# A Fourier mixing layer and its MLP on one core: the order of the one-channel loads, of the first sums and of the last results is changed

## The chip, the cores and the metric

One core of a Trainium2 chip runs the kernel. The metric is the time of one execution on the device in microseconds (us), as a median over runs. A core has four compute engines with an instruction queue each: TensorE (PE, matmul), VectorE (DVE), ScalarE (ACT) and GpSimd (POOL). SyncE (SP) only issues DMAs; ScalarE and POOL can issue DMAs too. Every queue is executed in order.

## The reference

```python
def reference(x, w_in, w_out):          # x: 8 x 3008 x 256, float32
    X = np.fft.fft(x, axis=1)           # along the sequence
    X = np.fft.fft(X, axis=2).real      # along the channels
    t = X.reshape(24064, 256)
    h = t @ w_in                        # 256 x 2048
    g = h * np.cos(h)
    return g @ w_out                    # 2048 x 256
```

## The kernel before, in words

*The channel DFT goes into the weights.* It is linear, so the kernel multiplies its matrices into `w_in` once: `fold_cos` and `fold_sin` (L293 to L306) make `Wc` and `Ws`, 128 x 2048 each, in four quarters of 512 columns. A quarter takes the two halves of `w_in` (`w1`, eight loads on SP's queue), two matmuls and one evacuation by ScalarE. Channel 128, the middle one, has a weight row of its own. It is row 127 of `Ws`. The step needs it as a column per 128 hidden units, so 16 DMAs of 128 elements turn it into `wex` (L299), four of them per quarter: those of quarters 0 to 2 on SP's queue, those of quarter 3 on ScalarE's.

*The sequence DFT is folded by symmetry.* For each batch, four tiles `xl0` to `xl3` (`load_x`, L169; `xl1` and `xl2` hold rows in reversed order and come by gathers on POOL's queue, `xl0` and `xl3` by three loads each on SP's) are added and subtracted into sums `e` and differences `o`, and these into `EO0` to `EO3` (`fold_x`, L325). VectorE does this for batch 0, POOL for the later batches, in small pieces (`FOLDS`) that stand between the steps below. A class `Dft` (L438) multiplies each `EO` by a constant matrix `MC`: `first` and `second` give two banks of PSUM, `side` copies half of one by ScalarE, `unfold` adds and subtracts on VectorE, and `plus` and `minus` (sums and differences) write the results for positions k and -k into rings of 8 tiles of 256 columns: `Rr` (real part), `Ir` (imaginary part). In each batch even and odd positions are separate DFTs (`R_even`, `I_even`, `R_odd`, `I_odd`).

*Channel 128 has its own ring `Rb`*, a single row spread over 128 partitions. For the even half of batch 0, `fold_first` (L380) spreads channel 128 of the loaded rows over 128 columns, and the DFT `x_even` gives `Rb` at once. For all the rest, `load_ext` (L540) reads channel 128 of all eight batches from DRAM, 4 bytes at a time, into `x1` (8 partitions x 768 elements, four times; five DMAs), writes it to DRAM as `xe_dr` and reads it back in tiles as `xs`. `fold_ext` (POOL) folds it, `clear_ext` and `dft_ext` run a small DFT of 28 matmuls between the steps, `ext_side` (ScalarE) copies the four groups out of PSUM, `ext_rows` makes one row per batch (VectorE the even half, POOL the odd half) and stores it to DRAM, and `spread_ext` loads a row into `Rb` with a broadcast DMA. `x1` and the row buffer share one tile (`rx`).

*The main work is 47 tiles of 256 positions (512 output rows), with 8 steps of 256 hidden units each: 376 steps.* The parts of step i are:
- `ext`: ScalarE writes `Rb` x `wex` into a PSUM bank `H`, two instructions (L661).
- `mm_P`, then `mm_Q`: four matmuls add `Wc` x `Rr` to it, four add `Ws` x `Ir`. `dbl` and `h_minus` give h for -k.
- `k_plus`, `k_minus`, `r_plus`, `r_minus`, two sines, `g_plus`, `g_minus`: h cos(h) in turns, on ScalarE and VectorE, into the tile `G`.
- `sum_1`, `sum_3`, `sum_2`, `sum_4`: four additions of 128 x 256 on POOL (`gtt`, L273).
- `mm_X1`, `mm_X2`: products with `w_out` or sums of its blocks (`WT`) into the banks `pA` to `pD`, which stand for a whole tile. Seven products serve for eight. The third product is the first that needs a POOL sum.

At the end of a tile `comb_copy`, `comb_1`, `comb_2`, `comb_22` and `comb_3` add the banks into `u` and `v`. `turn_u` and `turn_v` transpose these on VectorE, and `store` issues the output in pieces. For the last tile the stores go to SP's and ScalarE's queues in turns.

*The order.* Up to step 0 the program is written out by hand (before.py L943 to L979). From there each part is an event `at(time, function)`. A step's events stand PERIOD = 4.8 us apart (`T`), all events are sorted by time, and the functions run in that order. `pin` keeps an instruction in that program order on its engine. The loads of `load_x` and `spread_ext` are not pinned: the scheduler places them on SP's queue. The times only make the order, and the engines wait for each other by semaphores. The batch's folds begin at step 7 for batch 1; `load_ext` stands at -T, batch 1's `load_x` at -1.5 T, and the small DFT's events count from `e0`, 11 T.

The four helpers `mm` (L264), `vtt` (VectorE, L270), `gtt` (POOL, L273) and `act` (ScalarE, L276) issue most instructions, so the profile shows their lines.

Of the kernel before, what the change touches and what calls it, by code (L numbers as in the profile page):

```python
# [10 lines left out]
FP = mybir.dt.float32  # L11
# [4 lines left out]
ALU = mybir.AluOpType  # L16
# [3 lines left out]
ND = 256  # L20
# [83 lines left out]
def kernel(  # L104
# [45 lines left out]
    def gather_x(b, L, j, short):  # L150
# [13 lines left out]
            )  # L164
        )

    GATHERS = [(2, 0), (2, 1), (1, 0), (1, 1)]

    def load_x(b, gather=True):  # L169
        L = [  # L170
            spool.tile([128, 6 * ND], FP, tag=f"xl{j}", bufs=1, name=f"xl{j}")
            for j in range(4)
        ]
        if gather:
            for j, short in GATHERS:
                gather_x(b, L, j, short)
        for j, row in ((0, 0), (3, HALF)):
            nc.sync.dma_start(
                out=L[j][:, 0 : 4 * ND], in_=xrows(b, row, 4, 128, 4)
            )  # L180
            for h in range(2):
                nc.sync.dma_start(
                    out=L[j][64 * h : 64 * h + 64, 4 * ND :],
                    in_=xrows(b, row + 512 + 2 * h, 4, 64, 2),
                )
        return L
# [47 lines left out]

    Wc = cpool.tile([128, NDFF], FP, tag="Wc")
    Ws = cpool.tile([128, NDFF], FP, tag="Ws")
    wex = cpool.tile([128, NF], FP, tag="wex")

    halfpi2 = cpool.tile([128, 1], FP, tag="halfpi2")
    nc.vector.memset(halfpi2, 0.0)  # L240
# [35 lines left out]
        pin(nc.scalar.activation(out=o, in_=i, func=func, **kw))  # L276


    def fold_part(q, part, dst, tag):

        cols = slice(q * 512, (q + 1) * 512)
        ps = bank(tag)
        for h in range(2):
            mm(
                ps,
                CC[:, h * 256 + part : h * 256 + part + 128],
                w1_cols(h, q * 512, (q + 1) * 512),
                h == 0,
                h == 1,
            )  # L290
        act(dst[:, cols], ps)

    def fold_sin(q, tag="H"):  # L293
        fold_part(q, 128, Ws, tag)
        with nc.allow_non_contiguous_dma(reason="one row to columns"):
            for f in range(4 * q, 4 * q + 4):
                eng = nc.scalar if q == 3 else nc.sync
                pin(
                    eng.dma_start(  # L299
                        out=wex[:, f : f + 1], in_=Ws[127:128, f * 128 : (f + 1) * 128]  # L300
                    )
                )

    def fold_cos(q, tag="H"):
        fold_part(q, 0, Wc, tag)


    w2v = w2.rearrange("p (q c) -> p q c", c=ND)
# [71 lines left out]
    def fold_first(L):  # L380

        c = [t.rearrange("p (m d) -> p m d", d=ND)[:, :, 128:129] for t in L]
        c[1], c[2] = c[1][:, ::-1], c[2][:, ::-1]
        a = spool.tile([128, 6], FP, tag="xa", bufs=1, name="xa")
        g = spool.tile([128, 6], FP, tag="xg", bufs=1, name="xg")
        vtt(a.unsqueeze(2), c[0], c[1], ALU.add)
        vtt(g.unsqueeze(2), c[2], c[3], ALU.add)
        e = spool.tile([128, GW], FP, tag="G", bufs=3, name="xb")
        vtt(
            e[:, 0:768].rearrange("p (m d) -> p m d", d=128),  # L390
            a.unsqueeze(2).to_broadcast([128, 6, 128]),
            g.unsqueeze(2).to_broadcast([128, 6, 128]),
            ALU.add,
        )
        return e

# [39 lines left out]
            i += m  # L436

    class Dft:  # L438
        def __init__(self, ri, b, kodd, stat, ring=None, first=False):
            self.ri, self.b, self.kodd, self.stat = ri, b, kodd, stat  # L440
            self.n = NO if kodd else NE
            self.M = 127 if ri else 128
            self.first_only = first
            self.ring = ring if ring is not None else (Ir if ri else Rr)

        def mms(self, par, ps, start=True):
# [22 lines left out]
        def unfold(self):  # L469

            n = self.n
            self.ab = spool.tile([128, NE], FP, tag="ab", bufs=2, name="ab")
            n1 = n - 188
            u, v = self.uv[:, 0:NH], self.vs
            vtt(self.ab[:, 0:n1], u[:, 0:n1], v[:, 0:n1], ALU.add)
            u, v = (u, v) if self.ri == 0 else (v, u)
            vtt(self.ab[:, n - 1 : n - 189 : -1], u[:, 0:188], v[:, 0:188], ALU.subtract)
# [55 lines left out]
                )  # L533


    def spin(**kw):
        pin(nc.sync.dma_start(**kw))

    def load_ext():
        x1 = spool.tile([128, HALF + 1], FP, tag="rx", bufs=1, name="x1")  # L540
        xs = state["xs"] = spool.tile([128, 4, NB, 6], FP, tag="xs", bufs=1, name="xs")
        rows = [x1[j * NB : (j + 1) * NB] for j in range(4)]

        def copy(j, s0, s1, row, step):
            spin(
                out=rows[j][:, s0:s1],
                in_=bass.AP(
                    tensor=xt,
                    offset=x.offset + row * ND + 128,
                    ap=[[SEQ * ND, NB], [step * ND, s1 - s0], [1, 1]],  # L550
                ),
            )

        with nc.allow_non_contiguous_dma(reason="one channel, then runs of rows"):
            copy(1, 0, 1, 0, 1)
            copy(0, 0, 768, 0, 1)
            copy(1, 1, 768, SEQ - 1, -1)
            copy(2, 0, 768, HALF, -1)
            copy(3, 0, 768, HALF, 1)
            for j in range(4):  # L560
                spin(out=xe_dr[j], in_=rows[j][:, 0:768])
            for j in range(4):
                spin(
                    out=xs[:, j, :, 0:4],
                    in_=xe_dr[j][:, 0:512].rearrange("b (p m) -> p b m", m=4),
                )
                pairs = xe_dr[j][:, 512:768].rearrange("b (q h m) -> h q b m", h=2, m=2)
                for h in range(2):
                    spin(out=xs[64 * h : 64 * h + 64, j, :, 4:6], in_=pairs[h])
# [38 lines left out]

    def ext_rows(kodd, tt):
        n = NO if kodd else NE  # L610
        if not kodd:
            rx = spool.tile([128, HALF + 1], FP, tag="rx", bufs=1, name="rx")
            state["rx"] = rx[0:NB]
        rx, uv, b = state["rx"], state["side", 2 * kodd], state["side", 2 * kodd + 1]
        a = spool.tile([128, NE], FP, tag="ab", bufs=2, name="ab")[0:NB]
        n1 = n - 188
        u, v = uv[:, 0:NH], uv[:, NH:]
        tt(a[:, 0:n1], u[:, 0:n1], v[:, 0:n1], ALU.add)
# [37 lines left out]
    def ext(i):  # L656
        S = steps[i] = Step()
        S.H = bank("H")
        for j in range(2):
            f = 2 * (i % 8) + j  # L660
            act(S.H[:, j * TW : (j + 1) * TW], Rb[:, cols(i)], scale=wex[:, f : f + 1])  # L661

    def first_mm(i, W, ring, M):
        S = steps[i]
# [168 lines left out]
    def turn_v(q):  # L833
        turn(q, 2, tiles[q].v, 512, ((0, 0), (1, 1)))
        del tiles[q]

    def turn_u1(q):
        turn(q, 0, tiles[q].u[:, 0:TW], TW, ((1, 0),))

# [103 lines left out]
    for _ in range(8):  # L943
        mm(bank("M"), zero[:, 0:128], zero[:, 0:1].to_broadcast([1, 512]), True)
    sin(halfpi2)
    for q in range(2):
        fold_sin(q)
        fold_cos(q)
    EO, ops = fold_x(L_first, nc.vector, 1)

    def fold_now(keys):
        for key in keys.split():
            ops[key, 0]()

    R_even, I_even = Dft(0, 0, 0, EO[0]), Dft(1, 0, 0, EO[2])
    R_odd, I_odd = Dft(0, 0, 1, EO[1]), Dft(1, 0, 1, EO[3])

    fold_now("z1 z3 c0 e0 c3 e3 c2 e2 E2 x1 c1 e1 E0 EO0")
    fold_sin(2)
    fold_cos(2)  # L960
    R_even.first("pA")
    R_even.second("pB")
    xb = fold_first(L_first)
    fold_now("o0 o1 O0 o3 o2")
    R_even.side()
    x_even = Dft(0, 0, 0, xb, ring=Rb, first=True)
    x_even.first("pC")
    x_even.second("pD")
    R_even.unfold()
    R_even.plus()  # L970
    R_even.minus()
    fold_now("O2 EO2")
    I_even.first("pA")
    I_even.second("M")
    x_even.side()
    x_even.unfold()
    x_even.plus()
    x_even.minus()


    events = []
# [31 lines left out]
    for q in range(n_tiles):  # L1013
        t = (8 * q + 9) * T
        if q < n_tiles - 1:
            turns = ((2 * T + 1.0, turn_u), (3 * T + 1.0, turn_v))
        else:
            turns = ((4.3, turn_u1), (T + 1.15, turn_u2), (3 * T, turn_v))
        for dt, fn in (
            (1.45, comb_copy),  # L1020
            (4.2, comb_1),
            (T + 1.0, comb_2),
            (T + 1.1, comb_22),
            (T + 1.2, comb_3),
        ) + turns:
            at(t + dt, lambda fn=fn, q=q: fn(q))

# [27 lines left out]
    for t, fn in (  # L1055
        (-1.8, I_even.side),
        (-0.1, I_even.unfold),
        (0.0, I_even.plus),
        (0.1, I_even.minus),
        (0.95, lambda: fold_sin(3, "pD")),  # L1060
        (1.0, lambda: fold_now("EO1 EO3")),
        (3.0, lambda: fold_cos(3, "pA")),
        (3.1, lambda: R_odd.first("pB")),
        (3.2, lambda: R_odd.second("pC")),
        (T + 0.95, R_odd.side),
# [8 lines left out]
        (2 * T + 0.3, I_odd.minus),  # L1074
    ):
        at(t, fn)
    at(-T, load_ext)
    e0 = 11 * T
    at(e0 + 1.35, fold_ext)
    at(e0 + 2.905, clear_ext)  # L1080
    at(e0 + 4.75, dft_ext)
    for g in range(4):
        at(e0 + T * (1 + g // 2) + 1.46, lambda g=g: ext_side(g))
    at(e0 + 2 * T + 1.0, lambda: ext_rows(0, vtt))
    at(e0 + 3 * T + 1.35, lambda: ext_rows(1, gtt))
    at(e0 + 3 * T + 2.0, lambda: spread_ext(0, 1))
    fold_keys = [(k, p) for k in FOLDS for p in range(2 if k[0] not in "czx" else 1)]
    n_big = sum(k[0] not in "czx" for k, _ in fold_keys)
    for b in range(1, NB):
# [93 lines left out]
```

## Time and profile before

| | us |
|---|---|
| median of 5 runs | 1967.85 (1966.43 to 1976.26) |
| profiled execution | 1976.55 |
| its span | 1974.8 |
| TensorE busy | 1941.7 (98%) |
| first matmul of step 0 (`H<-Rr,Wc`) | 39.35 |
| small DFT of channel 128 (`H<-MC,xe`) | 113.11 |
| first `ext` from spread rows (`H<-Rb,wex` of step 16) | 140.59 |
| last `comb_3` | 1968.79 |

A line of the profile's timeline gives the start of a group of like instructions, its busy time, the engine, the line of the kernel, the operation, and `out<-in` by the names of the tiles with partitions x elements. The `x` at its end is the count. A bracket at the end, as in `[2.53 <-ACT H L276]`, is the time that the engine was idle just before the group, and what ended it. In a table by windows the columns after the window are its length, then busy time with the number of instructions of PE, DVE, ACT, POOL and weight loads, then the granted clock of TensorE (1 is full speed), the mean busy share of the core's 16 DMA engines, and GB/s. SPq is SP's DMA queue. A wait is put down to the releaser by semaphores, and a tile's name there can be that of another with the same semaphore.

### The profile page before, as it was taken

To read this page: it belongs to the slowest core of one execution; us is meant where nothing else is said; L and a number is where in the kernel's file an instruction comes from. 1 tells how busy PE (TensorE), PEld (TensorE's weight loads), DVE (VectorE), ACT (ScalarE), POOL (GpSimd) and SP (SyncE) were. 2 spreads that over 40 slices of the span, in tenths; PEclk is the share of its full clock that TensorE was granted. 3 is DMA by queue.
4 is the path that set the end of the run, shared out by engine and by line. 5 is a ranking of instruction groups with operands and counts; after the bars stand their busy time and mean duration, and the time that the engine had idled before them with its cause. 6 is when DMAs were issued, how large, how long until landed. Compare 5 with 4: busy or idle time off the path is not lost.

```text
span 1974.8 us, 28170 instructions
## 1 busy us (share of the span) xinstructions
PE 1941.7 (98%) x8855; PEld 1655.2 (84%) x8855; DVE 1417.4 (72%) x2348; ACT 1452.9 (74%) x2790; POOL 1349.8 (68%) x1853
## 2 busy tenths in 40 slices
PE   7989999999999999999999999999999999999998
PEld 4768888888888888888888888888888888887887
DVE  4657767777777767777677776777777776677777
ACT  1757767777777777777777776777777777777775
POOL 2767757776677766777677776677767776555654
PEclk9999999999999999999999999999999999999999
DMA  8821110111111011110210202002020110100101
GB/s 297 3 32 44 27 47 19 31 29 25 44 19 44 14 39 33 18 45 14 53 24 12 52 8 57 11 19 59 7 51 11 24 17 15 16 11 12 22 12 22
DMA packets 262401, 66.16 MB, mean 34 GB/s; under 512 B 249395, under 2 KB 252219, under 8 KB 262252
## 3 DMA queue, kind: packets, MB, share of 16 engines
q1 hardware_dynamic: 255916, 51.51, 14.9%
q0 software_dynamic: 3584, 12.58, 2.0%
q8 instruction: 70, 1.15, 0.3%
q14 instruction: 79, 0.65, 0.1%
q10 hardware_dynamic: 2752, 0.26, 0.1%
HBM read 39.48 MB, written 24.79 MB: 33 GB/s over the span
## 4 chain that ended last, share of the span: by engine, by line
PE 92%; DVE 3%; DMA 2%; ACT 2%; issue 1%; POOL 0%; SPq 0%; ACTq 0%; DVEq 0%; POOLq 0%
PE H L264 37%; PE pB L264 16%; PE pD L264 16%; PE pC L264 16%; PE pA L264 8%; DVE G L718 1%; ACT G L276 1%; DMA wex<-Ws 1%; DMA w<-in_moe_w_in_dram 1%; DVE v L270 0%; DVE G L270 0%; DVE M L270 0%; ACT E L276 0%; DVE ot L826 0%; DVE u L270 0%
## 5 line engine op out<-in xcount | busy, mean ns | idle before, releaser
L273 POOL TENSOR_TENSOR G<-G 128x256 f32<-128x256 f32 x1500 | 1079.2, 730 | 575.5 <-DVE G L718 473.0
L718 DVE SCALAR_TENSOR_TENSOR G<-H,G 128x512 f32<-128x512 f32 x376 | 257.0, 684 | 276.4 <-ACT G L276 276.4
L270 DVE TENSOR_TENSOR G<-H,G 128x512 f32<-128x512 f32 x376 | 260.0, 692 | 227.5 <-ACT G L276 224.4
L276 ACT ACTIVATE G<-H 128x512 int32<-128x512 f32 x376 | 224.6, 597 | 232.7 <-DVE G L270 231.3
L264 PE MATMUL H<-Rr,Wc 128*128 128x256 f32 x1504 | 388.5, 381 | 4.5 <-ACT H L276 4.4
L264 PE MATMUL pC<-G,WT 128*128 128x256 f32 x1504 | 387.9, 379 | 1.8 <-DVE u L270 1.6
L276 ACT ACTIVATE H<-Rb,wex 128x256 f32<-128x256 f32 x752 | 360.4, 479 | 39.0 <-DMA wex<-Ws 11.2
L264 PE MATMUL H<-Ir,Ws 127*128 127x256 f32 x1504 | 388.4, 380 | 0.7 <-ACT E L276 0.7
L276 ACT ACTIVATE E<-H 128x512 f32<-128x512 f32 x376 | 224.3, 596 | 207.4 <-PE H L264 204.7
L264 PEld LDWEIGHTS H<-Rr,Wc 128*128 128x128 f32 x1504 | 284.3, 190 | 53.7 <-ACT H L276 7.4
L264 PEld LDWEIGHTS pC<-G,WT 128*128 128x128 f32 x1504 | 284.5, 190 | 45.5 <-PE H L264 5.1
L264 PEld LDWEIGHTS H<-Ir,Ws 127*128 127x128 f32 x1504 | 283.0, 190 | 45.1 <-ACT E L276 6.1
L276 ACT ACTIVATE G<-G,halfpi 128x512 f32<-128x512 f32 x376 | 269.5, 717 | 1.5 <-DVE G L270 1.5
L270 DVE TENSOR_TENSOR G<-E,H 128x512 f32<-128x512 f32 x376 | 255.3, 679 | 5.3 <-PE H L264 3.4
L270 DVE TENSOR_TENSOR M<-G,M 128x512 f32<-128x512 f32 x376 | 257.7, 685 | 0.0
L718 DVE SCALAR_TENSOR_TENSOR G<-G,M 128x512 f32<-128x512 f32 x376 | 254.2, 676 | 0.4 <-ACT M L276 0.3
L276 ACT ACTIVATE M<-M,halfpi 128x512 f32<-128x512 f32 x376 | 246.4, 655 | 0.4 <-DVE M L270 0.3
L264 PE MATMUL pB<-G,WT 128*128 128x256 f32 x752 | 227.3, 384 | 2.4 <-POOL G L273 2.4
L264 PE MATMUL pA<-G,w 128*128 128x256 f32 x752 | 223.7, 379 | 2.4 <-issue 2.4
L276 ACT ACTIVATE M<-G 128x512 int32<-128x512 f32 x376 | 224.1, 596 | 0.0
L264 PE MATMUL pD<-G,WT 128*128 128x256 f32 x752 | 223.7, 379 | 0.0
L264 PE MATMUL pD<-G,w 128*128 128x256 f32 x752 | 223.7, 379 | 0.0
(129 smaller groups left out, 1788.3 us busy)
## 6 DMA issues: line engine op xcount, KB each, us to landing
out_dram<-ot SPq DMA_DIRECT2D x496, 32.0 KB
xl<-in_x_dram SPq DMA_DIRECT2D x16, 512.0 KB
xl<-in_x_dram SPq DMA_DIRECT2D x32, 128.0 KB
out_dram<-ot SPq DMA_DIRECT2D x256, 2.0 KB
MC<-dft_mats SPq DMA_DIRECT2D x4, 943.5 KB
Rb<-r SPq DMA_DIRECT2D x10, 376.0 KB
w<-in_moe_w_in_dram SPq DMA_DIRECT2D x4, 512.0 KB
w<-in_moe_w_out_dram SPq DMA_DIRECT2D x1, 2048.0 KB
```

The source lines that it names most:

```text
L264: nc.tensor.matmul(out_, lhsT=lhsT, rhs=rhs, start=start, stop=stop, skip_group_check=True)
L270: pin(nc.vector.tensor_tensor(out=o, in0=a, in1=b, op=op))
L273: pin(nc.gpsimd.tensor_tensor(out=o, in0=a, in1=b, op=op))
L276: pin(nc.scalar.activation(out=o, in_=i, func=func, **kw))
L718: nc.vector.scalar_tensor_tensor(out=o, in0=h, scalar=TWO_PI, in1=c, op0=ALU.mult, op1=ALU.mult)
```

## The change

It has seven parts.

1. *`wex`* becomes four tiles, one per quarter. Its copies come right behind each quarter of `Ws`: those of quarters 0 and 1 on ScalarE's queue, those of 2 and 3 on POOL's. The evacuation of `Wc`'s last quarter gets a time of its own (4.81).
2. *`fold_first`* adds channel 128 on VectorE in its small form and spreads it over 128 columns with ScalarE.
3. *Batch 0's DFTs*: `O2` and `EO2`, on which `I_even` waits, come ahead of `R_even`'s unfold; `o0` comes early; the sums (`plus`) of `R_even` and `x_even` stay ahead of step 0, while their differences, those of `I_even`, and `EO3` become events between 0.2 and 4.7. These two DFTs unfold into the buffers `xt0`, and the tile `ab` is a little wider.
4. *Eight warm matmuls* of zeros (`warm(8)`) stand behind the second quarter's fold.
5. *The one-channel loads*: `load_ext` stands at -1.5 T, ahead of batch 1's `load_x`, and its DRAM turn (`turn_ext`: `xe_dr`, then `xs`) at -T. `load_x`'s loads on SP are now pinned.
6. *The small DFT* begins a step later (`e0` = 12 T). The odd half goes first: VectorE makes its rows, its spread follows at once, and POOL makes the even half a step later.
7. *The last tile's* `v` is added, transposed and stored in two halves (`end_v`).

```diff
+    def spin(**kw):
+        pin(nc.sync.dma_start(**kw))
+
     def load_x(b, gather=True):
         for j, row in ((0, 0), (3, HALF)):
-            nc.sync.dma_start(
-                out=L[j][:, 0 : 4 * ND], in_=xrows(b, row, 4, 128, 4)
-            )
+            spin(out=L[j][:, 0 : 4 * ND], in_=xrows(b, row, 4, 128, 4))
             for h in range(2):
-                nc.sync.dma_start(
+                spin(
...
-    wex = cpool.tile([128, NF], FP, tag="wex")
+    wex = [cpool.tile([128, 4], FP, tag=f"wex{q}", name=f"wex{q}") for q in range(4)]
...
     def fold_sin(q, tag="H"):
-        fold_part(q, 128, Ws, tag)
-        with nc.allow_non_contiguous_dma(reason="one row to columns"):
-            for f in range(4 * q, 4 * q + 4):
-                eng = nc.scalar if q == 3 else nc.sync
-                pin(
-                    eng.dma_start(
-                        out=wex[:, f : f + 1], in_=Ws[127:128, f * 128 : (f + 1) * 128]
-                    )
-                )
+        ps = fold_mms(q, 128, tag)
+        act(Ws[:, q * 512 : (q + 1) * 512], ps)
+        eng = nc.gpsimd if q > 1 else nc.scalar
+        for f in range(4):
+            c = q * 512 + f * 128
+            pin(eng.dma_start(out=wex[q][:, f : f + 1], in_=Ws[127:128, c : c + 128]))
...
     def fold_first(L):
         vtt(a.unsqueeze(2), c[0], c[1], ALU.add)
         vtt(g.unsqueeze(2), c[2], c[3], ALU.add)
+        vtt(a, a, g, ALU.add)
         e = spool.tile([128, GW], FP, tag="G", bufs=3, name="xb")
-        vtt(
+        act(
             e[:, 0:768].rearrange("p (m d) -> p m d", d=128),
             a.unsqueeze(2).to_broadcast([128, 6, 128]),
-            g.unsqueeze(2).to_broadcast([128, 6, 128]),
-            ALU.add,
         )
...
+            tag = "xt0" if self.early else "ab"
+            self.ab = spool.tile([128, 2 * NH], FP, tag=tag, bufs=2, name=tag)
...
     def load_ext():
             copy(3, 0, 768, HALF, 1)
+            state["rows"] = rows
+
+    def turn_ext():
+        rows, xs = state["rows"], state["xs"]
             for j in range(4):
                 spin(out=xe_dr[j], in_=rows[j][:, 0:768])
...
     def ext_rows(kodd, tt):
-        if not kodd:
+        if kodd:
             rx = spool.tile([128, HALF + 1], FP, tag="rx", bufs=1, name="rx")
...
+    def end_v(q):
+        T = tiles[q]
+        for h in range(2):
+            c = slice(h * TW, (h + 1) * TW)
+            vtt(T.v[:, c], T.v[:, c], T.acc[3][:, c], ALU.add)
+            turn(q, 2 + h, T.v[:, c], TW, (((0, 0), (1, 1))[h],))
...
+    def warm(n):
+        w = bank("M")
+        for _ in range(n):
+            mm(w, zero[:, 0:128], zero[:, 0:1].to_broadcast([1, 512]), True)
+
     for q in range(2):
         fold_sin(q)
         fold_cos(q)
+    warm(8)
...
-    fold_now("z1 z3 c0 e0 c3 e3 c2 e2 E2 x1 c1 e1 E0 EO0")
+    fold_now("z1 z3 c0 e0 o0 c3 e3 c2 e2 E2 x1 c1 e1 E0 EO0")
...
-    fold_now("o0 o1 O0 o3 o2")
+    fold_now("o1 O0 o3 o2")
...
+    fold_now("O2 EO2")
     R_even.unfold()
     R_even.plus()
-    R_even.minus()
-    fold_now("O2 EO2")
...
     x_even.plus()
-    x_even.minus()
...
-            turns = ((2 * T + 1.0, turn_u), (3 * T + 1.0, turn_v))
+            turns = ((T + 1.2, comb_3), (2 * T + 1.0, turn_u), (3 * T + 1.0, turn_v))
         else:
-            turns = ((4.3, turn_u1), (T + 1.15, turn_u2), (3 * T, turn_v))
+            turns = ((4.3, turn_u1), (T + 1.15, turn_u2), (T + 1.2, end_v))
...
-        (0.1, I_even.minus),
-        (1.0, lambda: fold_now("EO1 EO3")),
-        (3.0, lambda: fold_cos(3, "pA")),
+        (1.0, lambda: fold_now("EO1")),
+        (1.1, I_even.minus),
+        (3.0, lambda: state.update(wc3=fold_mms(3, 0, "pA"))),
+        (4.81, lambda: act(Wc[:, 1536:2048], state.pop("wc3"))),
+        (0.2, R_even.minus),
+        (0.3, x_even.minus),
+        (4.7, lambda: fold_now("EO3")),
...
-    at(-T, load_ext)
-    e0 = 11 * T
+    at(-1.5 * T, load_ext)
+    at(-T, turn_ext)
+    e0 = 12 * T
...
-    for g in range(4):
-        at(e0 + T * (1 + g // 2) + 1.46, lambda g=g: ext_side(g))
-    at(e0 + 2 * T + 1.0, lambda: ext_rows(0, vtt))
-    at(e0 + 3 * T + 1.35, lambda: ext_rows(1, gtt))
-    at(e0 + 3 * T + 2.0, lambda: spread_ext(0, 1))
+    for n, g in enumerate((2, 3, 0, 1)):
+        at(e0 + T * (1 + n // 2) + 1.46, lambda g=g: ext_side(g))
+    at(e0 + 2 * T + 1.0, lambda: ext_rows(1, vtt))
+    at(e0 + 2 * T + 1.02, lambda: spread_ext(0, 1))
+    at(e0 + 3 * T + 1.35, lambda: ext_rows(0, gtt))
```

More of the change, by code (lines that the diff above doesn't have):

```diff
@@ L276, in act, with fold_mms @@
         pin(nc.scalar.activation(out=o, in_=i, func=func, **kw))
-    def fold_part(q, part, dst, tag):
-        cols = slice(q * 512, (q + 1) * 512)
+    def fold_mms(q, part, tag):
         ps = bank(tag)
@@ L290, in fold_part @@
             )
-        act(dst[:, cols], ps)
+        return ps
     def fold_sin(q, tag="H"):
-        fold_part(q, 128, Ws, tag)
-        with nc.allow_non_contiguous_dma(reason="one row to columns"):
-            for f in range(4 * q, 4 * q + 4):
-                eng = nc.scalar if q == 3 else nc.sync
-                pin(
-                    eng.dma_start(
-                        out=wex[:, f : f + 1], in_=Ws[127:128, f * 128 : (f + 1) * 128]
-                    )
-                )
+        ps = fold_mms(q, 128, tag)
[4 more added lines that the diff above has]
+            pin(eng.dma_start(out=wex[q][:, f : f + 1], in_=Ws[127:128, c : c + 128]))
     def fold_cos(q, tag="H"):
-        fold_part(q, 0, Wc, tag)
+        ps = fold_mms(q, 0, tag)
+        act(Wc[:, q * 512 : (q + 1) * 512], ps)
     w2v = w2.rearrange("p (q c) -> p q c", c=ND)
@@ L438, with __init__ @@
     class Dft:
-        def __init__(self, ri, b, kodd, stat, ring=None, first=False):
+        def __init__(self, ri, b, kodd, stat, ring=None, first=False, early=False):
             self.ri, self.b, self.kodd, self.stat = ri, b, kodd, stat
@@ L443, in __init__ @@
             self.first_only = first
+            self.early = early
             self.ring = ring if ring is not None else (Ir if ri else Rr)
@@ L471, in unfold @@
             n = self.n
-            self.ab = spool.tile([128, NE], FP, tag="ab", bufs=2, name="ab")
+            tag = "xt0" if self.early else "ab"
+            self.ab = spool.tile([128, 2 * NH], FP, tag=tag, bufs=2, name=tag)
             n1 = n - 188
@@ L533, in minus_sum @@
                 )
-    def spin(**kw):
-        pin(nc.sync.dma_start(**kw))
     def load_ext():
@@ L559, in load_ext @@
             copy(3, 0, 768, HALF, 1)
+            state["rows"] = rows
+    def turn_ext():
+        rows, xs = state["rows"], state["xs"]
+        with nc.allow_non_contiguous_dma(reason="runs of rows"):
             for j in range(4):
@@ L614, in ext_rows @@
         rx, uv, b = state["rx"], state["side", 2 * kodd], state["side", 2 * kodd + 1]
-        a = spool.tile([128, NE], FP, tag="ab", bufs=2, name="ab")[0:NB]
+        a = spool.tile([128, 2 * NH], FP, tag="ab", bufs=2, name="ab")[0:NB]
         n1 = n - 188
@@ L660, in ext @@
             f = 2 * (i % 8) + j
-            act(S.H[:, j * TW : (j + 1) * TW], Rb[:, cols(i)], scale=wex[:, f : f + 1])
+            act(S.H[:, j * TW : (j + 1) * TW], Rb[:, cols(i)], scale=wex[f // 4][:, f % 4 : f % 4 + 1])
     def first_mm(i, W, ring, M):
@@ L953, in fold_now @@
             ops[key, 0]()
-    R_even, I_even = Dft(0, 0, 0, EO[0]), Dft(1, 0, 0, EO[2])
+    R_even, I_even = Dft(0, 0, 0, EO[0], early=True), Dft(1, 0, 0, EO[2])
     R_odd, I_odd = Dft(0, 0, 1, EO[1]), Dft(1, 0, 1, EO[3])
-    fold_now("z1 z3 c0 e0 c3 e3 c2 e2 E2 x1 c1 e1 E0 EO0")
+    fold_now("z1 z3 c0 e0 o0 c3 e3 c2 e2 E2 x1 c1 e1 E0 EO0")
     fold_sin(2)
@@ L963 @@
     xb = fold_first(L_first)
-    fold_now("o0 o1 O0 o3 o2")
+    fold_now("o1 O0 o3 o2")
     R_even.side()
-    x_even = Dft(0, 0, 0, xb, ring=Rb, first=True)
+    x_even = Dft(0, 0, 0, xb, ring=Rb, first=True, early=True)
     x_even.first("pC")
     x_even.second("pD")
+    fold_now("O2 EO2")
     R_even.unfold()
     R_even.plus()
-    R_even.minus()
-    fold_now("O2 EO2")
     I_even.first("pA")
@@ L1023 @@
             (T + 1.1, comb_22),
-            (T + 1.2, comb_3),
         ) + turns:
```

## The prediction

> **What bounds the kernel now.** I read the page first, then who waited for whom on TensorE, then the timeline around each wait, the DMA share by window, and last the order of the built program on each queue.
>
> ```profile
> PE 1941.7 (98%) x8855; PEld 1655.2 (84%) x8855; DVE 1417.4 (72%) x2348; ACT 1452.9 (74%) x2790; POOL 1349.8 (68%) x1853
> ...
> PE H L264 <- POOL xe L273: 5.6, 1, 5.6
> PE H L264 <- ACT H L276: 4.4, 4, 2.5
> ```
>
> TensorE (PE) is busy 98% of the span; from 146 us to 1964 us a step without a DFT takes 4.75 us of matmuls, which this change does not touch. What it can win lies in the first 146 us and the last 7.
>
> ```profile
> 38.30 0.99 ACT L276 ACTIVATE H<-Rb,wex 128x256 f32<-128x256 f32 x2 [7.59 <-DMA wex<-Ws]
> 39.35 2.04 PE L264 MATMUL H<-Rr,Wc 128*128 128x256 f32 x4 [2.53 <-ACT H L276]
> ...
> 47.72 36.30 SPq L537 DMA_DIRECT2D x<-in_x_dram  x5
> ...
> 84.13 17.78 SPq L537 DMA_DIRECT2D xe_dr<-x  x4
> ...
> 84.81 0.19 POOL L351 COPY e<-xl 128x6 f32<-128x6 f32 x1
> 84.97 1.94 POOL L330 TENSOR_TENSOR e<-xl 128x381 f32<-128x381 f32 x2
> 86.87 3.02 POOL L273 TENSOR_TENSOR G<-G 128x256 f32<-128x256 f32 x4
> 89.87 0.59 PE L264 MATMUL pB<-G,WT 128*128 128x256 f32 x2
> ...
> 112.30 0.39 POOL L273 TENSOR_TENSOR xs<-xs 128x96 f32<-128x96 f32 x1 [6.42 <-DMA out_dram<-ot]
> 113.11 4.18 PE L264 MATMUL H<-MC,xe 128*8 128x189 f32 x28 [5.61 <-POOL xe L273]
> ...
> 140.59 0.99 ACT L276 ACTIVATE H<-Rb,wex 128x256 f32<-128x256 f32 x2 [4.39 <-DMA Rb<-r]
> ```
>
> Step 0 waits for the `wex` copies; step 12's small DFT waits for the one-channel data (the named `out_dram` shares a semaphore with `xs`); step 16 waits for the spread of `Rb`. The POOL rows at 84.81 fold batch 1's first tile, between the sums of steps 5 and 6.
>
> ```profile
> 38.00:40.00 2.00, 0.65 (x2) 0.57 (x3) 0.43 (x2) 1.20 (x3) 1.92 (x6) 0.85 0.82 230
> 50.00:52.00 2.00, 1.31 (x7) 0.83 (x6) 1.86 (x4) 2.00 (x6) 0.00 (x0) 1.00 0.19 1
> 52.00:62.00 10.00, 7.64 (x30) 5.85 (x29) 6.91 (x14) 5.59 (x11) 6.48 (x11) 0.89 0.91 3
> 84.00:98.00 14.00, 14.00 (x66) 12.29 (x66) 9.62 (x16) 10.96 (x22) 12.20 (x19) 1.00 0.96 2
> 100.00:102.00 2.00, 2.00 (x11) 1.73 (x11) 1.90 (x4) 1.35 (x3) 0.53 (x2) 1.00 0.02 6
> ```
>
> The last two columns are DMA share and GB/s: big loads fill the engines to about 40 us, then the one-channel stream holds them from 51 to 98.4, 47.4 us at 2 to 4 GB/s.
>
> **The change, part by part.** *The start.* Ahead of `EO2` VectorE loses `o0` (0.91, now in its idle time before 17.95), the spread (0.96, now ScalarE's: 0.6 for 512 columns in its rows, so 0.9 for 768, in a stretch where it idles 0.74 and the user at 27.18 is later) and `R_even`'s unfold, sums and differences (0.61 + 1.00 + 0.15, now behind). `EO2` moves from 33.3 to 29.8; `I_even`, free to start when `x_even`'s matmuls end at 30.84, gains 2.5; `Rb`'s sums are ready at 32.2, ScalarE's first step at 33.2, and step 0 follows `I_even` at 34.3 instead of 39.35. The differences (0.5 + 0.15 + 0.5), `EO3` (0.95) and `I_even`'s differences come later, in front of step 0's own VectorE work, where that engine idles 1.8 and 4.6 us. Step 3 is 4 to 6.5 us earlier; I take 5. The 8 warm matmuls cost 8 x 0.63 = 5.0 at half clock, 2.5 at full, in a 2.56 us gap; were they to overrun, `pA` still waits for VectorE until 24.2. The gap of 2.53 before 39.35 was followed by matmuls of 2.04 instead of 1.03, the one of 2.54 at 30.84 by no slow ones. The Trainium skill ("TensorE: Matmul & The Clock Gate", "Why this matters for your kernels") sees the clock drop after gaps of more than about 3 us; by that the warm matmuls would win nothing, and the sum would not move.
>
> *The copies of `wex`.* Twelve leave SP (26.03 to 40.9) for ScalarE (8) and POOL (4), and four go from ScalarE to POOL. ScalarE's eight take 0.74 each, 5.9 us, between 11.3 and 20, where it idles; its `Wc` evacuations queue behind them, which nothing needs before 19. POOL's take 0.95 each by its gather row (0.6 to 1.6): four inside its 22.5 us of idleness before 30, four more in its 13.0 us before 53.86. But each hardware DMA takes the next of eight completion semaphores and is not issued before that semaphore's last DMA has landed; two rows show it:
>
> ```profile
> SPq L225 <- DMA xl<-in_x_dram: 5.6, 3, 2.5
> SPq L299 <- DMA MC<-dft_mats: 4.3, 2, 2.5
> ```
>
> In the new order the fourth `w1` load on SP gets the semaphore of ScalarE's third copy, and the first `MC` load that of the fourth. So SP holds that load and all behind it until the copy, issued at 12.6, has landed; what is queued before keeps the engines busy to about 18.4, and data follow an issue by 1.9 (`xl`'s at 41.01 and 42.9). At the early end it lands as fast as the small `r` write at 134.90 (1.6 us), and nothing runs dry. At the late end the group, begun at 11.4, needs what SP's needed from 26.03 (12.2 us) and lands at 23.6: 23.6 + 1.9 - 18.4 = 7.1 us of hold. It has a queue of its own but saturated loads beside it (DMA share 1.0 to 34 us), so it lands when they thin out: I take 19.0, a hold of 2.5 us. The Trainium skill ("DMA: Bandwidth & Descriptors", "Issuing engines are not separate DMA queues") speaks against the move: another engine's queue saves issue time alone. By that the late end holds, and the sum below is 4.6 us worse. No row shows such a copy under this load.
>
> *Batch 1's rows behind the one-channel stream.* This is the part that decides. Both are on SP's queue, and the stream now comes first. Its start: big loads and gathers end at 40.1 today; minus 0.6 idle, plus 2.5 of hold, 42.0 (38 to 46.6). Its length: 47.4 (the four loads' issues were let through after 9.4, 11.1, 12.8 and 13.6 us; four at the first rate make 38, four at the last 55). It ends at 89.4. The first `xl` tile is three loads; SP issues them about 0.55 apart at the end, the last data come 1.9 after its issue: landed 2.9 later, 92.3. POOL wants it at 84.81 - 5 = 79.8. It is an in-order queue, so step 6's four sums stand behind that fold: copy and fold 2.1, three sums 2.2, and the third product of step 6, today at 89.87, runs at 96.7: +6.8. A gap of some 11 us then costs half clock for about 3.7 us after it, as after 113.11 and 39.35: +1.8. At that point the kernel is 8.6 us behind, whatever the start had gained.
>
> *The one-channel DFT.* The stream's data, today in `xs` 15 us after it ends, are there at 105, and the DFT, a step later, asks at 119: no wait. Step 11 starts at 102.40 and step 17 at 146.49, 44.1 us; six steps of 4.75 and the DFT at full clock (half of 4.18) make 30.6, so 13.5 is lost there (the 5.61 gap, half clock to 117.9, 0.55, 1.83 and 1.25 of later gaps). Of this, VectorE's rows (0.9) and POOL's second half beside its sums (1.5) stay; the odd spread, first now and no longer behind two other spreads, comes in time to 0.3 (0 to 1.5). Gain 13.5 - 2.7 = 10.8; I take 10.4 (9 to 11.5), as POOL's step 11 now holds fold and copies together (2.5 + 3.03 against 4.75).
>
> *The end.* Today a 0.65 addition, a 0.71 transpose and four 0.45 issues on each queue follow one another from 1968.79. In halves, the second transpose ends at 1970.5 instead of 1970.2, but two issues follow instead of four: -0.7 (-1.0 to 0).
>
> *Loads of batches 2 to 7* are pinned and come 10 to 19 steps later, next to the `Rb` spreads, six issues of 0.55. POOL's first use stays 5 to 13 steps (24 to 62 us) away, and the slowest such load today needed 9: 0.
>
> **Sum**: +8.6 - 10.4 - 0.7 = -2.5 us. The profiled execution took 1976.55 (span 1974.8), 8.7 above the median of the five runs; taken as a difference, 1967.85 becomes **1965.4**. In short, the end of the stream minus 91.9.
>
> **The rivals.** *A, the rows come in time* (17%): if the stream is fast (four loads at 9.4: end 80), the row wait shrinks; with none, -5 - 10.4 - 0.7 = -16.1, 1951.8. For it: nothing else uses the queue. Against: its last three loads were slower each time. Halfway, 1958.
>
> *B, slower: the stream ends later* (17%). Every us of it is one of the kernel; from an end at 97.8 the result is over 5.9 us above before. Four loads at the slowest rate (55) on 42: 97, +5; with the hold at its late end 101.6, +9.7, 1977.6. For it: the trend 9.4 to 13.6, gathers in its first us, copies of `wex` among loads. Against: nothing else runs in most of it.
>
> *C, the DFT's gain is not there* (9%): the odd spread or POOL keeps the old loss; half the 10.4 back gives 1970.6, all of it 1975.8.
>
> *D, the pinned loads stall later batches* (4%): six batches at, say, one hidden POOL wait of 2 us each, +12: 1977. Against: 24 us of cover.
>
> **How the numbers follow.** The likeliest case has 53%, its own range 1961.5 to 1970.5 (stream ending 85.5 to 94.5). About 0.3% (5.9 us) is what a measurement of this kernel tells from no change. Faster: 7% of the likeliest and 16% of A; slower: 2% of the likeliest, 13% of B, 5% of C, 3% of D; the rest within. The 8-in-10 range reaches to half of A and, on the other side, to where B's two prices lie about evenly around it: 1957.5 to 1975.
>
> **What would show it.** Right: ScalarE's first `Rb` step without a `wex` wait near 33 to 36; POOL idle 10 to 14 us ahead of `e<-xl`, released by `xl<-in_x_dram`, near 92, with a PE gap of about 11 before `pB<-G,WT`; no gap before `H<-MC,xe`; SP's fourth `w1` issue near 19. Wrong: DMA share falling before 86 or after 95, no POOL wait at all, or a wait for `Rb` above 2 us.

## The result and the profile after

The changed kernel is slower: a median of 1979.05 us (1972.4 to 1985.69, 31 runs) against 1968.86 us (1965.76 to 1982.58, 52 runs) in the same comparison; the ratio is 1.0042, with a 95% interval of 1.0032 to 1.0053. The forecast was 1965.4 with a range of 1957.5 to 1975. The profiled execution took 1982.35 us, its span is 1980.6.

The waits of the kernel after, in us in all, times, and the longest:

```profile
PE pB L265 <- POOL G L274: 21.0, 3, 18.6
...
POOL e L349 <- DMA xl<-in_x_dram: 19.5, 1, 19.5
...
ACT H L277 <- DMA Rb<-r: 0.6, 1, 0.6
```

The first line was 2.4 us before the change, in two waits of at most 1.8; its 18.6 is new, and the second line is the cause: POOL stands for 19.5 us before it can fold batch 1's first tile, and TensorE's third product stands behind POOL. The last line was 4.4 us before the change: the odd spread is now in time. The timeline of after shows where these lie:

```profile
33.30 0.99 ACT L277 ACTIVATE H<-Rb,wex 128x256 f32<-128x256 f32 x2 [2.11 <-DVE Rb L271]
...
35.70 1.03 PE L265 MATMUL H<-Rr,Wc 128*128 128x256 f32 x4
...
80.69 13.70 SPq L168 DMA_DIRECT2D xl<-in_x_dram  x6
...
98.22 0.19 POOL L349 COPY e<-xl 128x6 f32<-128x6 f32 x1 [19.49 <-DMA xl<-in_x_dram]
98.37 1.93 POOL L328 TENSOR_TENSOR e<-xl 128x381 f32<-128x381 f32 x2
100.27 3.00 POOL L274 TENSOR_TENSOR G<-G 128x256 f32<-128x256 f32 x4
...
102.52 1.22 PE L265 MATMUL pB<-G,WT 128*128 128x256 f32 x2 [18.58 <-POOL G L274]
...
127.81 2.09 PE L265 MATMUL H<-MC,xe 128*8 128x189 f32 x28
```

The first `ext` waits for VectorE and no longer for `wex`; step 0 starts 3.65 us earlier. SP begins to issue batch 1's rows at 80.69, but the queue takes the first of the six loads only at 91.4; within the 13.70 us of the group the first one blocks for 10.7. This moment, at which SP's queue takes the next load, is called the end of the stream below. The small DFT has no bracket: it waits for nothing. The windows (length, then PE, DVE, ACT, POOL and weight loads as in the prediction, granted clock, DMA share, GB/s) show the end of the one-channel stream and what TensorE's clock does meanwhile:

```profile
82.00:84.00 2.00, 1.94 (x9) 1.35 (x8) 1.29 (x2) 1.49 (x4) 0.00 (x0) 1.00 1.00 3
84.00:86.00 2.00, 0.00 (x0) 0.00 (x0) 1.29 (x2) 1.74 (x4) 0.00 (x0) 1.00 0.81 3
...
88.00:90.00 2.00, 0.00 (x0) 0.00 (x0) 0.00 (x0) 0.00 (x0) 0.00 (x0) 0.50 0.94 2
90.00:92.00 2.00, 0.00 (x0) 0.00 (x0) 0.00 (x0) 0.00 (x0) 0.00 (x0) 0.50 0.42 1
92.00:94.00 2.00, 0.00 (x0) 0.00 (x0) 0.00 (x0) 0.00 (x0) 0.00 (x0) 0.50 0.86 221
94.00:96.00 2.00, 0.00 (x0) 0.00 (x0) 0.00 (x0) 0.00 (x0) 0.00 (x0) 0.50 0.81 223
96.00:98.00 2.00, 0.00 (x0) 0.00 (x0) 0.00 (x0) 0.00 (x0) 0.00 (x0) 0.50 1.02 294
```

Until 92 the engines move 1 to 3 GB/s; then the rows come, 221 to 294 GB/s for 6 us. Step starts (`H<-Rr,Wc`) in the two profiles give the account:

| | before | after | after less before |
|---|---|---|---|
| step 0 | 39.35 | 35.70 | -3.65 |
| step 4 | 69.14 | 63.04 | -6.10 |
| third product of step 6 | 89.87 | 102.52 | +12.65 |
| step 9 | 92.90 | 108.53 | +15.63 |
| step 11 | 102.40 | 118.04 | +15.64 |
| step 17 | 146.49 | 152.73 | +6.24 |
| last product begins | 1967.21 | 1973.35 | +6.14 |
| span | 1974.8 | 1980.6 | +5.8 |

The start won 6.1, the wait for the rows turned that into a loss of 15.6, the small DFT gave 9.4 back, and in the 1820 us after it the two kernels differ by 0.1.

### The profile page after: what moved, and what is told of

Same layout as the page of the kernel before. It is cut to its first block, busy times and chain, and to the rows that moved or that the text cites. A ratio compares the mean times of both kernels' runs of the same rounds, so it can differ in the third digit from the quotient of the medians.

```text
span 1980.6 us, 28191 instructions
## 1 busy us (share of the span) xinstructions
PE 1941.1 (98%) x8863; PEld 1654.9 (84%) x8863; DVE 1416.7 (72%) x2349; ACT 1452.7 (73%) x2791; POOL 1351.8 (68%) x1862
## 4 chain that ended last, share of the span: by engine, by line
PE 92%; DVE 3%; ACT 1%; issue 1%; POOL 1%; SPq 0%; DMA 0%; DVEq 0%; POOLq 0%
PE H L265 37%; PE pB L265 16%; PE pC L265 16%; PE pD L265 16%; PE pA L265 8%; DVE G L719 1%; ACT G L277 1%; DVE v L271 0%; POOL G L274 0%; DVE G L271 0%; SPq L168 0%; DMA xl<-in_x_dram 0%; ACT E L277 0%; DVE M L271 0%; DVE u L271 0%
## 5 line engine op out<-in xcount | busy, mean ns | idle before, releaser
L277 ACT ACTIVATE H<-Rb,wex 128x256 f32<-128x256 f32 x752 | 360.1, 479 | 26.3 <-DVE G L719 10.4
```

## The experiments

*The theories.* R: the loss is the place of batch 1's rows behind the one-channel stream, and the end of that stream sets the time. H, the rival: the loss is in the start, where ScalarE's `wex` copies hold loads back. F, a second question that the medians raise: the profiled execution of before may not be typical, so that its wait at the small DFT is not there to be won in most executions. Ratios are to before on the same chip in the same comparison; before's own medians there were 1968.9 to 1973.9.

**Undoing one part: rows first.**

```diff
-    at(-1.5 * T, load_ext)
+    at(-1.4 * T, load_ext)
```

> The kernel after, with the one-channel loads moved behind batch 1's row loads again; nothing else is undone. Theory R (the loss is batch 1's rows standing behind the one-channel stream on SP's queue): the rows land near 50 us, POOL does not wait for `xl`, and the 21.7 us that TensorE lost at step 6 (gap of 18.6, half clock 3.1) are gone. The stream starts about 4 us later than after's (1.5 MB at some 400 GB/s), ends near 96, `xs` is there near 107, and the small DFT asks near 103: a new gap of 4 to 7 there, with half clock 6 to 9 in all. So 13 to 16 us less than after: 1963 to 1966, just under before. Rival H (the loss sits in the start, the copies of `wex` and the hold on the loads): nothing changes, 1977 to 1981.

Measured: 1964.79 us median (1961.31 to 1971.12), ratio 0.9974 (0.9956 to 0.9993). The order of eleven loads on one queue decides between slower and faster. The gap at step 6 is gone (POOL's fold has no wait before it); the DFT has a small one, below the forecast 4 to 7, as the stream let the next issue go at 94.7:

```profile
79.68 0.19 POOL L349 COPY e<-xl 128x6 f32<-128x6 f32 x1
...
108.57 2.32 PE L265 MATMUL H<-MC,xe 128*8 128x189 f32 x28 [1.45 <-POOL xe L274]
```

**Taking the wait away and leaving the traffic: batch 1's folds later.**

```diff
-        f0 = max(7, s0 - 1)
+        f0 = max(12, s0 - 1)
```

> The kernel after, with batch 1's folds on POOL begun at step 12 instead of 7; the loads stay in after's order. Theory R: the rows still land near 98, but POOL asks for them near 103 and waits for nothing; the 21.7 us at step 6 are gone. `xs` comes behind the rows, near 109, and the small DFT asks near 103: a gap of 6 to 8, with half clock 8 to 10 in all. 11 to 14 us less than after, 1965 to 1968. Rival H: the loss stays, 1977 to 1981. If the rows cost by their traffic and not by POOL's wait, the loss stays too.

Measured: 1964.13 us (1962.08 to 1974.72), ratio 0.9971 (0.9952 to 0.9991). In its profile the stream ends at 84 and the rows come from then to about 93, later than POOL asks for them in after (78.7); here POOL asks at 104 and waits for nothing:

```profile
104.32 0.20 POOL L349 COPY e<-xl 128x6 f32<-128x6 f32 x1
...
107.29 2.21 PE L265 MATMUL H<-MC,xe 128*8 128x189 f32 x28
```

TensorE is busy all of the time from 84 to 94, while the rows come at up to 222 GB/s. So it is POOL's wait that cost, not the traffic. The expected gap at the DFT did not come in the profiled execution, as the stream ended early.

**The part alone, in the kernel before.** Only part 5 is applied: `load_ext` at -1.5 T, `turn_ext` at -T, `load_x`'s loads pinned.

> The kernel before, with part 5 of the change alone: the one-channel loads ahead of batch 1's rows, and these pinned behind them. Theory R: the stream starts near 41 to 44 (after's starts at 44), ends 82 to 91, the rows land 6.8 later, 89 to 98, and POOL asks at 85: TensorE is 4 to 13 late, plus 1 to 3 of half clock, and the small DFT does not wait. Slower than before: 1972 to 1980, a gap of 5 to 13 before `pB<-G,WT` of step 6. As the end of the stream sets the time, the early start of after has been swallowed: this comes within 4 of after (1979), not 5 or more above it. Rival H (the loss is in the start's parts): no slower than before, 1964 to 1970.

Measured: 1978.37 us (1974.96 to 1992.57), ratio 1.0050 (1.0028 to 1.0073). One part of seven makes a loss as large as the whole change's:

```profile
97.25 0.19 POOL L352 COPY e<-xl 128x6 f32<-128x6 f32 x1 [16.23 <-DMA xe_dr<-x]
...
101.56 1.22 PE L265 MATMUL pB<-G,WT 128*128 128x256 f32 x2 [15.35 <-POOL G L274]
```

(The name in the first bracket shares a semaphore with `xl`.) Its step 8 starts at 84.32, after's at 82.05, and yet the third product of step 6 runs at 101.56 here and at 102.52 there: the lead of the start is swallowed. H, by which this kernel would be no slower than before, is refuted.

**The kernel after once more.** Nothing is edited.

> The kernel after, unchanged, for a second profiled execution. Theory R: its span and that of the first (1980.6, stream ending at 91.4, third product of step 6 at 102.5) differ by as much as the ends of their streams, to within 2 us.

Measured: 1974.54 us, span 1972.8.

```profile
71.40 15.30 SPq L168 DMA_DIRECT2D xl<-in_x_dram  x6
...
90.80 0.19 POOL L349 COPY e<-xl 128x6 f32<-128x6 f32 x1 [12.19 <-DMA xl<-in_x_dram]
...
95.10 1.22 PE L265 MATMUL pB<-G,WT 128*128 128x256 f32 x2 [11.30 <-POOL G L274]
```

The first of these loads was taken at 83.7, 7.7 us earlier than in the first profile; the span is 7.8 shorter. The rest of the kernel is the same in both: from the third product to the end of the span 1878.1 and 1877.7 us. So the difference of these two executions is that of their streams' ends, and the spread of after's times (13 us) should be the same thing in more executions. From a start near 44 the same five loads took some 47 us in one execution and 40 in the other.

**All `wex` copies on POOL.**

```diff
-        eng = nc.gpsimd if q > 1 else nc.scalar
+        eng = nc.gpsimd
```

> The kernel after, with all 16 `wex` copies on POOL, so that none of ScalarE's copies holds the fourth `w1` load on SP. Theory R: the engines for DMA hardly ran dry (share 0.90 from 10 to 20 us, 1.01 after), so the stream starts at most 2 us earlier and each of these is one of the kernel's: 0 to 3 less than after, 1976 to 1979. Rival H (the hold is what costs): 7 or more less.

Measured: 1976.86 us (1971.18 to 1980.06), ratio 1.0022 (1.0005 to 1.0040). The hold on SP is gone (the fourth `w1` load goes at 8.2). It is worth 2.2 us by the medians, which is within R's 0 to 3, and 3.9 by the ratios; the two kernels were measured in different comparisons, and the intervals of their ratios overlap. Both are far from H's 7 or more. The queue's own waits in after show the size of the hold, 4.5 us before the fourth `w1` load, which was issued at 17.73:

```profile
SPq L207 <- DMA wex<-Ws: 4.5, 1, 4.5
```

In the four profiles in which POOL waits for the rows (after twice, part 5 alone, and this one) the stream ends at 91.4, 83.7, 90.1 and 86.4, and the third product of step 6 follows 11.1 to 11.7 us later, whatever the start had won.

**Halving the stream, in after and in before.** Each one-channel load takes pairs of channels from half the rows. Part of channel 128's rows is left out.

```diff
+            n = (s1 - s0) // 2
...
-                    ap=[[SEQ * ND, NB], [step * ND, s1 - s0], [1, 1]],
+                    ap=[[SEQ * ND, NB], [step * ND, n], [1, 2]],
```

> The kernel after, with its one-channel loads fetching two neighbouring channels of half the rows, so half as many pieces of 8 bytes; the rest is as in after (it leaves out half of channel 128's rows, so channel 128's part of the output is of other numbers). Theory R: the stream takes 24 us instead of 47, ends near 68, the rows land near 74, before POOL asks (79): the whole 21.7 us at step 6 are gone, no wait at the small DFT either: 1957 to 1960, and the spread of its times (1972 to 1986 in after) shrinks to under 9, as the stream no longer ends on the path. Rival H (the loss is in the start): 1977 to 1981.

> The kernel before, with the same halved one-channel loads (the same part left out). Theory R with the profiled execution taken as typical: the wait at the small DFT goes with its half clock, 8 to 10 less than before, near 1960. Rival F (most executions of before wait little at the DFT): 0 to 5 less, 1965 to 1969, which with the first run's 1.4 permille of part 6 alone would say that the profiled execution had shown a loss that the median does not have.

Measured: after's 1961.58 us (1959.69 to 1964.48), ratio 0.9948 (0.9929 to 0.9967); before's 1966.51 us (1964.14 to 1967.87), ratio 0.9964 (0.9946 to 0.9982). Both lose their spread (13 to 5 us, and 17 to 4), so the stream is what spreads both. After's 17.5 us are somewhat less than the 19 to 22 of the expectation. Before's floor is 1966.5, a time within F's 1965 to 1969. In the comparison of the result about half of before's executions lie there already (25 of 52 under 1968.5): those wait little, the others up to 16 us. That is F, for that half. How large the half is differs by comparison: in the three of this section it is 29 of 91, and in the one at hand, where before's median was 1973.9, it is 8 of 35. So by ratio the halving wins 7.1 us here, between F's 0 to 5 and R's 8 to 10. In the profile of before with halved loads the DFT waits for nothing:

```profile
106.66 2.09 PE L264 MATMUL H<-MC,xe 128*8 128x189 f32 x28
```

Its steps 11 to 17 take 35.9 us, against 44.1 in the profiled execution of before and 34.7 in after: of the 9.4 won there, 8.2 are the late stream, and part 6 itself is worth 1.2. Without a late stream, the whole change is worth 4.9 us (1966.51 less 1961.58), most of it, by the profiles, the early start.

**The small DFT's part alone, in before.** Only part 6 is applied (`e0` = 12 T, odd half first on VectorE).

> The kernel before, with part 6 of the change alone: the small DFT a step later, odd half first. Theory R with the profiled execution of before taken as typical: `xs` is there when the DFT asks, and the 9.4 us between steps 11 and 17 that the change won in the profiles are won here: 6 to 9.4 less than before, 1959 to 1963. Rival F (most executions of before have a shorter stream than the profiled one and do not wait at the DFT): 0 to 4 less, 1965 to 1969, and the slow tail of before's times (1975 to 1982) goes.

Measured: 1968.15 us (1965.03 to 1978.47), ratio 0.9986 (0.9965 to 1.0007): 2.8 us less, with an interval of 6.9 less to 1.4 more. The middle is in F's range (0 to 4); the interval leaves 6 just possible and excludes the 9.4 for the median. In its profile the DFT waits for nothing:

```profile
113.45 2.09 PE L264 MATMUL H<-MC,xe 128*8 128x189 f32 x28
```

**The kernel before once more.**

> The kernel before, unchanged, for a second profiled execution. Theory R with the first profile as typical: a gap of 4 to 6 us before the first `H<-MC,xe`, stream ending near 98, span near 1975. Rival F: at a span near 1965 the gap there is under 1 us and the stream ends before 93.

Measured: 1973.67 us, span 1971.9, and a wait again:

```profile
110.94 4.18 PE L264 MATMUL H<-MC,xe 128*8 128x189 f32 x28 [5.37 <-POOL xe L273]
```

It is another execution above the floor (by 7 us), with the stream ending at 95.7. The gap is as R said, the end 2 us earlier; F's condition, a span near 1965, was not met, so this run tells nothing of the executions at the floor. What is said of them rests on the halved streams and on the distribution of the times.

**Rows first, with the small DFT of before.** `e0` is 11 T again, the even half first.

> The kernel rows_first with the small DFT as before has it (11 T, even half first): the early start and the stream, without part 6. The DFT asks some 5 us earlier than before's (the start's lead) and 4.75 earlier than rows_first's, while the stream ends at 84 to 95 as there. The lead turns into the wait: 3 to 8 slower than rows_first (1964.8), 1968 to 1973, that is no faster than before, with a gap of 4 to 10 before `H<-MC,xe`. If part 6 is worth only the 1.2 that the two kernels with halved loads show between steps 11 and 17: 1965 to 1967.

Measured: 1968.32 us (1963.13 to 1975.38), ratio 0.9987 (0.9968 to 1.0006), 3.5 above rows_first by the medians of two comparisons, though the intervals of the ratios overlap; the gap is 3.42, just under the forecast 4.

```profile
105.42 3.58 PE L265 MATMUL H<-MC,xe 128*8 128x189 f32 x28 [3.42 <-POOL xe L274]
```

In this profile the early start meets the stream at the DFT instead. With part 6 (rows first, above) that gap was 1.45.

**Rows first, without the warm matmuls.**

```diff
-    warm(8)
```

> The kernel rows_first without the eight warm matmuls. If they keep the clock up, the half clock near 20 to 27 us grows or begins earlier, and it is 1 to 3 slower than rows_first (1964.8): 1966 to 1968. If they only fill a gap that the loads set, it is the same within 1: 1964 to 1966.

Measured: 1964.45 us (1960.73 to 1972.84), ratio 0.9966 (0.9947 to 0.9986): the same as with them (1964.79). In the profiles the clock is halved from 19.3 to 26.2 with them and from 20.8 to 27.6 without, 6.8 to 6.9 us each.

**A version that waits for neither.** The DRAM turn stands ahead of batch 1's rows, the folds begin at step 14, all copies of `wex` are on POOL.

```diff
-        eng = nc.gpsimd if q > 1 else nc.scalar
+        eng = nc.gpsimd
...
-    at(-T, turn_ext)
+    at(-1.5 * T + 0.05, turn_ext)
...
-        f0 = max(7, s0 - 1)
+        f0 = max(14, s0 - 1)
```

> The kernel after, with three changes: the turn of the one-channel data through DRAM stands right behind their loads, ahead of batch 1's rows; batch 1's folds on POOL begin at step 14; all `wex` copies are on POOL. Theory R: stream from 41 to between 80 and 90, `xs` there 8 to 10 later, before the DFT asks (102); rows by 96 to 106, before POOL asks (near 110). No wait on any of it in any execution: as a_pairs (1961.6), or 1 to 2 less for the earlier start: 1959.5 to 1962, and a spread under 7. If the rows come after 110, a gap before a third product shows it.

Measured: 1961.42 us (1959.01 to 1963.15), ratio 0.9950 (0.9931 to 0.9969). It is faster than both kernels, and its spread is 4 us. Its stream ended at 85.4, and neither the DFT nor batch 1's fold stands on a load:

```profile
102.93 0.39 POOL L274 TENSOR_TENSOR xs<-xs 128x96 f32<-128x96 f32 x1
...
105.88 2.09 PE L265 MATMUL H<-MC,xe 128*8 128x189 f32 x28
...
115.11 0.20 POOL L349 COPY e<-xl 128x6 f32<-128x6 f32 x1
```

## Why the prediction was wrong, point by point

By the medians the change cost 10.2 us (1979.05 less 1968.86), where a gain of 2.5 was forecast. The prediction's short form was "the end of the stream minus 91.9", that is 1965.4 with an end at 89.4, one us for one. The two profiles of after have ends at 91.4 and 83.7. The form gives 1967.4 and 1959.7; they took 1982.35 and 1974.54, 15.0 and 14.9 more. So the slope was right and the constant was 15 us off. The first end was within the likeliest case (85.5 to 94.5), the second came before 86, which the prediction had named as a sign of being wrong. The constant splits into four terms:

- **The base: 8.7.** "The profiled execution took 1976.55 (span 1974.8), 8.7 above the median of the five runs; taken as a difference, 1967.85 becomes 1965.4." This step failed first. The sum took 10.4 us of waiting out of an execution that stood above the median because of that waiting, and then moved the difference to a median, 1967.85, that lies 1.3 above the floor and has almost none of it. The excess can be named: 8.2 at the DFT by comparison with the halved stream (44.1 less 35.9), and 1.7 between steps 2 and 3, which took 9.03 instead of 7.35 with a half clock from 59.9 to 63.3. That makes 9.9, and 1976.55 less 9.9 is 1966.6, the floor.
- **The landing of the rows: 3.9.** "Landed 2.9 later" measured 6.8 (91.4 to 98.22) and 7.1 (83.7 to 90.80). The 1.9 us was the time from an issue to its first data. Of six loads, 1.5 MB, the first tile's three must be complete, and at the 221 to 223 GB/s of 92 to 96 their 768 KB alone take about 3.5 us. The term had no transfer time in it.
- **The half clock: 1.2.** From the third product to step 9 it is 6.0 us instead of before's 3.0, so 3.0 was lost and not 1.8.
- **The DFT and the end: 1.0 and 0.4.** Steps 11 to 17 gave 9.4 instead of 10.4, in the profiles; the tail gave 0.34 of 0.7 (from the last product's begin to the span's end 7.59 and 7.25).

These make 15.2, and POOL's fold and sums took 4.3 where 4.4 were counted, which leaves 15.1 against the 15.0.

*Right.* The place and chain of the wait: POOL at `e<-xl`, released by the rows, the third product of step 6 behind it. The lead swallowed: third products at 101.56 and 102.52 from starts 2.3 us apart. The sizes of that wait were forecast for an end at 89.4: POOL idle 10 to 14, a gap of about 11 on TensorE. They were 19.5 and 18.6 with the end at 91.4, and 12.2 and 11.3 with the end at 83.7. The stream's length, 47.4 from before, was met in the first profile; in the second it was 40, so a part of this hit is luck. The start: 5 forecast, 6.1 in the profiles (1.7 of which is before's half clock), and 4.9 as the whole change's worth without the stream. The hold by ScalarE's third `wex` copy: the fourth `w1` load at 17.73, forecast 19.0, with the late end at 23.6. The late end was the prediction's reading of the Trainium skill ("DMA: Bandwidth & Descriptors", "Issuing engines are not separate DMA queues"), which says that another engine's queue saves only the time of issuing. That reading did not come true: the copy, issued at 12.6, was done by 17.7, beside loads at a DMA share of 0.90. The warm matmuls are worth nothing in the time, as was said. The reason given for it, the threshold of about 3 us of the Trainium skill ("TensorE: Matmul & The Clock Gate", "Why this matters for your kernels"), is not what the runs show: the clock halves near 20 us beside a gap of 0.98 (with the warm matmuls) as after one of 3.17 (without), and in before at 59.9 after one of 2.36. Whether such thin matmuls count as work for the clock is not shown by any run here.

*The rivals.* A, the rows in time, had the price of 1951.8; with the halved stream it measures 1961.6. Of the 10 us between, 9.2 are again the DFT's gain that before's floor does not have to give (10.4 counted, 1.2 found). B's side came true and its mechanism did not: ends of 83.7 and 91.4 stand against its 97. C, the gain at the DFT missing, is half the truth and for another reason: the spread of `Rb` waits 0.6 and the gain is there in the profiles (9.4), but an execution at before's floor had only 1.2 of it to win. D does not show: from step 17 to the last product it is 1820.72 us in before and 1820.62 in after.

The range ended at 1975, and the slower side had 23%. With the transfer time of the rows, and with the floor as base and only the floor's gain at the DFT, the same sum gives 1966.5 + 8.6 + 3.9 - (10.4 - 8.2) - 0.7 = 1976.1.

## What to carry to other kernels

A profiled execution that is 0.4% above the median has its excess somewhere: find it before you take a wait out of that profile and credit the median with it. When a transfer is moved behind another on an in-order queue, its time is the release of the queue, plus the issues, plus its own bytes at the measured rate, and whoever asks first must ask after that; here a later asker (folds at step 12 or 14) was as good as an earlier load. A lead won ahead of such a wait is worth nothing until the wait is gone.

## What the runs showed of the hardware that was not expected

- The same 24 thousand 4-byte pieces took 40 to 47 us in two executions of the same program (let go at 83.7 and at 91.4, with the start near 44 in both). Before's times are bunched at 1966 to 1968 with a tail to 1982, since an end of the stream that is early enough wins it nothing more; after's are spread over 1972 to 1986, since there every us counts.
- An issue on SP can block for long: the third one-channel load held SP for 22.3 us (29.77 to 52.06), and `xl`'s first for 10.7. The line of an issue in a timeline starts where it blocks: the group of `xl` starts at 80.69, and its data from 92 on.
- A half clock came without a long gap: in the profile of rows_first from 132.0 to 135.4 after a gap of 1.96 (128.6 to 130.6), in late_turn from 53.0 to 56.4 after one of 2.37 (50.1 to 52.4), and in all fourteen profiles but one a stretch begins between 18 and 24 us. After the gaps of 11 to 19 us at step 6 it began 2.9 to 4.0 us after the last matmul and lasted 4.5 to 5.9 us beyond the next.
